# Forgetting attention with a gated FFN on one core: shared output chunks, stacked last tokens, a new order, and x of three batches turned by DMA

## The chip, the cores and the metric

One core of a Trainium2 chip runs the whole program. The metric is device time in microseconds, median of several runs. The five engines have instruction streams of their own: TensorE (PE, with its weight loads listed as PEld), VectorE (DVE), ScalarE (ACT), GpSimd (POOL) and SyncE (SP), which here only issues DMAs.

## The reference

For 8 batches, 8 heads, 576 tokens and a head dimension of 64, attention with a decay made from a gate `f`, and behind it an FFN with a gated convolution over the tokens:

```python
def _attn_ref(q, k, v, f):
    scores = scale * np.matmul(q, k.transpose(0, 1, 3, 2))
    cum = np.cumsum(np.log(np.clip(f, 0.0001, 1.0)), axis=-1)
    decay = cum[:, :, :, None] - cum[:, :, None, :]
    scores = np.where(causal, -1000000000.0, scores + decay)
    attn = softmax(scores)
    return np.matmul(attn, v)

def _moe_ref(x, w_in, conv_w, w_out):      # x: (8, 576, 512), the heads side by side
    h = np.maximum(x @ w_in, 0.0)          # d_ff = 1024
    conv_out = sum(conv_w[k] * shifted(h, k - 1) for k in range(3))
    gate = 1.0 / (1.0 + np.exp(-conv_out))
    return h * gate @ w_out
```

## The kernel before, in words

**Units of work.** Attention runs over 16 half batches `hb` (4 heads of a batch each), the FFN over 8 batches `b` and 8 blocks of 128 hidden features `ff`. The 576 tokens are four blocks of 128 and one of 64 (`SL`), the last tokens.

**Attention of a half batch.** q and k come transposed by DMA (L229, `q`), the rows of the decay are added to the operands (`rw`, `fi`), so that one matmul gives scores with decay. For each pair of heads, `sd` makes the four diagonal blocks, `so` the rest for one head, `st` the last 64 x 64 for all four (all in L362); `ed`, `eo`, `et` are the exponentials on ACT (L403, L420, L382). For half batches 0 to 7 a mask is added by a matmul (L370), for the rest POOL selects (`md`, `mt`: L406, L385). `va` casts v and adds a column of ones (L266, L268). `pv` (L438) multiplies: for query block n and head h it adds over key blocks m <= n, with the exponentials as weights (128 x 128) and 65 columns of v, so that the 65th column is the sum of the row. It has three parts of two, two and one query blocks, 12, 28 and 20 matmuls; the last query block is 128 rows wide and starts at token 448, so half of its rows repeat block 3. `n` (L445, L446) divides by the sums, in three parts. `t` turns the result by ten transposes on PE (L454) and `tx` copies it to `xt` on ACT or DVE (L459).

**FFN of a batch.** `f` (L468) is eight matmuls of 288 columns for one ff; `r` a relu on ACT (L478); `c` and `d` the convolution on DVE (L483, L485); `a` a tanh on ACT (L488); `g` the gate on DVE (L492). `o` (L499) multiplies with w_out: 128 tokens by 512 outputs, added over 8 ff. For the last 64 tokens (L503) the 512 outputs are split in two halves of 256, with 64-wide weights that go to two halves of the array, 16 matmuls a batch. `e` copies the result out of PSUM, `s` stores it, SP issuing (L525, L528).

**What sets the order.** Every task has a name such as `sd5` or `o3.2`; the string `ORDER` lists them all, some with the engine (`tx4@ACT`). `Plan.play` walks it and emits the instructions, so each engine's stream is the sub-sequence of its tasks, and the buffers (PSUM `ps`, 4; `xm`, 2; `xt`, 2; q/k `qk`, 4; and so on) are given out in that order. SP's queue is such a stream too: a DMA whose data aren't there yet holds all the DMAs behind it. Across engines only the semaphores of true dependences order the work.

**The start.** The gate `f` comes in two copies, one issued by ACT and one by SP (L271, L272); `dca`, `dcl`, `dcs`, `dck` make the decay and `ki` writes it to a DRAM image (L328). q and k of half batches 0 and 1 are loaded plain (`ld`, L208), turned on PE (`tp`, L215) and copied (`cl`, L221 on ACT, L223 on DVE).

Of the kernel before, what the change touches and what calls it, by code (L numbers as in the profile page):

```python
# [7 lines left out]
FP32 = mybir.dt.float32  # L8
FP16 = mybir.dt.float16
# [8 lines left out]
cw dca ld0 ld0.1.1 dcl dcs ld0.0.0 ld1 ld0.0.1 tp0.0.0 cl0.0.0@ACT cwt ld0.1.0 tp0.0.1 tp0.1.0 tp0.1.1 ld1.0.0 tp1.0.0  # L18
dck cl0.0.1@ACT cl0.1.0@DVE cl0.1.1@ACT cl1.0.0@ACT ld1.0.1 tp1.0.1 q2.0 cl2.0 cl1.0.1@ACT sd0 ed0 tp1.1.0 tp1.1.1
cl1.1.1@ACT ki@SP q2.1 sd1 so0.0 eo0.0 ed1 so1.1 eo1.1 so1.0 v0.0 v0.3 cl1.1.0@DVE rw1 so0.1 eo1.0 eo0.1 v0.4 v0.2  # L20
v0.1 sd3 ed3 so3.0 sd2 eo3.0 ed2 cl2.1 wi0 rw2 wi1 wic1@POOL so2.1 va1.0@DVE eo2.1 st0 et0 va0.0@DVE va0.1@DVE pv0.0
n0.0 so2.0 st1 et1 eo2.0 pv0.1 so3.1 pv0.2 eo3.1 va1.1@ACT sd5 q3.1 n0.1 n0.2 pv1.0 q3.0 wi3 n1.0 pv1.1 n1.1 pv1.2
n1.2 ed5 so5.1 eo5.1 cl3.1 wic0@POOL t0 tx0@ACT t1 tx1@DVE cl3.0 wi2 wic3@POOL q5.0 sd4 ed4 rw3 so4.1 eo4.1 f0.0 r0.0
f0.1 f0.2 f0.3 q5.1 v1.0 r0.1 v1.1 v1.2 v1.3 va2.0@POOL c0.0 d0.0 c0.1 wic2@ACT q4.1 r0.3 d0.1 so4.0 f0.4 c0.3 r0.2
c0.2 d0.3 eo4.0 h0 sd7 sd6 so5.0 a0.0 g0.0 a0.1 g0.1 r0.4 ed7 c0.4 d0.4 so7.0 eo5.0 cl5.1 so7.1 ed6 f0.5 cl5.0 a0.4
r0.5 v1.4 c0.5 rw5 eo7.1 wo1 st3 et3 eo7.0 a0.3 va2.1@POOL d0.2 woc1@POOL so6.0 d0.5 g0.4 st2 et2 f0.6 r0.6 eo6.0
so6.1 eo6.1 cl4.1 pv2.0 n2.0 pv2.1 va3.0@ACT a0.2 va3.1@ACT n2.1 f0.7 pv2.2 n2.2 g0.2 r0.7 c0.7 sd11 ed11 sd10 ed10
pv3.0 pv3.1 pv3.2 n3.0 so11.1 t2 n3.1 n3.2 q4.0 so10.1 wo2 d0.7 c0.6 cl4.0 a0.5 g0.5 eo11.1 wo0 eo10.1 tx2@ACT t3
tx3@ACT g0.3 d0.6 wo3 so11.0 eo11.0 a0.7 g0.7 so10.0 eo10.0 f1.0 f1.1 r1.0 c1.0 f1.2 d1.0 f1.3 q6.0 cl6.0 a0.6
woc2@POOL r1.1 st5 woc3@POOL r1.2 g0.6 rw4 et5 sd8 r1.3 c1.3 q6.1 woc0@ACT f1.4 q7.0 h1 a1.0 r1.4 sd9 ed9 d1.3 v2.0  # L30
o0.0 o0.1 so8.0 ed8 c1.4 cl6.1 d1.4 a1.3 c1.1 g1.3 a1.4 g1.4 cl7.0 g1.0 e0.0@ACT st4 et4 f1.5 eo8.0 r1.5 c1.5 d1.5
so8.1 eo8.1 so9.0 eo9.0 f1.6 f1.7 r1.7 so9.1 r1.6 v2.2 v2.1 v2.3 v2.4 eo9.1 va5.0@POOL va5.1@DVE va4.0@ACT rw6
va4.1@ACT pv5.0 pv5.1 pv5.2 n5.0 n5.1 n5.2 sd12 ed12 d1.1 c1.7 sd13 ed13 a1.1 pv4.0 n4.0 pv4.1 so12.1 pv4.2 t5 n4.1
n4.2 a1.5 so13.1 eo12.1 v3.0 v3.1 q7.1 t4 tx4@ACT o0.2 d1.7 tx5@DVE a1.7 c1.2 d1.2 g1.5 v3.3 eo13.1 q9.0 so12.0 eo12.0
o0.3 cl7.1 v3.2 a1.2 c1.6 d1.6 e0.1@ACT g1.1 a1.6 f2.0 r2.0 g1.7 g1.6 f2.1 f2.2 c2.0 r2.1 d2.0 rw7 g1.2 so13.0 r2.2
c2.2 eo13.0 o0.4 st7 et7 f2.3 sd15 q9.1 h2 a2.0 r2.3 e0.2@ACT va6.0@DVE va7.0@DVE so15.1 so15.0 pv6.0 zc ed15 eo15.1
f2.4 r2.4 eo15.0 v3.4 f2.5 sd14 q8.1 v4.0 so14.0 n6.0 c2.3 ed14 o1.0 st6 g2.0 eo14.0 d2.2 so14.1 a2.2 s0.2 o1.1
va6.1@DVE eo14.1 pv7.0 c2.1 et6 r2.5 e1.0@ACT fi9 d2.1 c2.4 d2.4 v4.2 d2.3 g2.2 a2.3 s0.1 q8.0 n7.0 f2.6 r2.6 sd18
sd19 ed19 c2.5 a2.4 pv6.1 pv6.2 d2.5 n6.1 n6.2 s1.0 fi8 g2.4 a2.5 va7.1@POOL pv7.1 pv7.2 v4.1 ed18 f2.7 n7.1 n7.2
q10.0 a2.1 g2.1 g2.3 r2.7 t6 so19.1 tx6@DVE c2.7 eo19.1 t7 v4.3 q11.0 tx7@ACT c2.6 d2.6 o1.2 f3.0 st9 md19 d2.7 f3.1  # L40
r3.0 a2.6 et9 o1.3 q11.1 c3.0 g2.6 r3.1 c3.1 a2.7 d3.1 st8 et8 sd17 e1.1@ACT ed17 f3.2 r3.2 md18 mt9 d3.0 g2.7 so19.0
# [67 lines left out]
def kernel(  # L109
# [601 lines left out]
```

## Time and profile before

| | us |
|---|---|
| three runs | 255.52, 256.81, 257.61 |
| median | 256.81 |
| span of the profiled execution | 254.4 |
| PE busy | 235.6 (93%) |
| ACT busy | 217.4 (85%) |
| DVE busy | 216.8 (85%) |
| POOL busy | 45.9 (18%) |

Of the profiled execution the page gives the span from its first instruction to its last, 254.4 us, and no other time; the runs' median stands beside it. The profile page gives for each engine the busy time, a line of 40 slices, the chain of work that ended last, and groups of instructions by line of the kernel. A group's mean duration of a matmul holds its latency; matmuls overlap one another, so steps between starts are shorter.

### The profile page before, as it was taken

What the parts mean: (1) busy time and instruction counts of PE and PEld (TensorE: products, weight loads), DVE (VectorE), ACT (ScalarE), POOL (GpSimd) and SP (SyncE); (2) the same over time, 40 slices, a digit from 0 to 9 for tenths busy, and PEclk for the clock granted to TensorE, in tenths of its full rate; (3) what the DMA queues carried; (4) which work ended last, traced back from release to release, by engine and by line L of the source; (5) the groups of instructions that cost most, each with busy time, mean ns of one, the idle gap of its engine ahead of it and who ended that gap; (6) DMA issues with size and microseconds to landing.
All of it is one profiled execution on the core that took longest, in us unless ns stands there. A gap on an engine that the chain in (4) does not pass through costs nothing.

```text
span 254.4 us, 6767 instructions
## 1 busy us (share of the span) xinstructions
PE 235.6 (93%) x2784; PEld 171.8 (68%) x2784; DVE 216.8 (85%) x353; ACT 217.4 (85%) x295; POOL 45.9 (18%) x79
## 2 busy tenths in 40 slices
PE   1899979779898999999999999999999999999992
PEld 1887766467656867687766886688767867875541
DVE  7631667969998999999989889889998999999961
ACT  4779858998999999897999799998999999796841
POOL 8100202022202401011104130245104302000000
PEclk9999999999999999999999999999999999999999
DMA  6979999999899979999998999999999802020335
GB/s 181 304 163 225 225 208 172 196 198 293 210 193 207 260 124 230 213 253 208 212 259 247 200 179 213 230 238 174 223 236 270 251 23 80 5 84 1 103 112 180
DMA packets 114695, 48.24 MB, mean 190 GB/s; under 512 B 104034, under 2 KB 105250, under 8 KB 114664
## 3 DMA queue, kind: packets, MB, share of 16 engines
q1 hardware_dynamic: 114370, 47.14, 85.4%
q8 instruction: 22, 0.36, 0.6%
q0 software_dynamic: 208, 0.51, 0.6%
q10 hardware_dynamic: 86, 0.16, 0.2%
q14 instruction: 9, 0.07, 0.1%
HBM read 21.11 MB, written 10.17 MB: 123 GB/s over the span
## 4 chain that ended last, share of the span: by engine, by line
PE 57%; DVE 15%; DMA 9%; SPq 7%; ACT 5%; issue 4%; POOL 0%; DVEq 0%; POOLq 0%; ACTq 0%
PE ps L468 14%; PE ps L499 14%; PE ps L362 12%; PE ps L438 9%; DVE u L483 5%; DVE hg L492 4%; SPq L258 4%; DMA vf<-in_v_dram 4%; DVE u L485 3%; DMA hg<-in_k_dram 3%; PE ps L454 2%; PE ps L503 2%; DMA qk<-in_k_dram 2%; ACT pp L420 2%; PE ps L370 2%
## 5 line engine op out<-in xcount | busy, mean ns | idle before, releaser
L420 ACT ACTIVATE pp<-ps 128x1024 f16<-128x1024 f32 x64 | 65.0, 1038 | 6.6 <-PE ps L362 4.9
L468 PE MATMUL ps<-xt,w_in_f 128*128 128x288 f16 x512 | 68.9, 286 | 1.8 <-ACT xt L459 0.8
L362 PE MATMUL ps<-qk 128*128 128x128 bf16 (+2 forms) x576 | 63.6, 240 | 1.6 <-ACT ht L478 1.1
L499 PE MATMUL ps<-w_out_f,hg 128*128 128x512 f16 x256 | 59.9, 379 | 0.1
L468 PEld LDWEIGHTS <-w_in_f 128*128 128x128 f16 x512 | 48.8, 98 | 15.8 <-issue 2.5
L483 DVE SCALAR_TENSOR_TENSOR u<-ht,cwt 128x576 f32<-128x576 f16 x64 | 54.8, 862 | 2.8 <-ACT ht L478 2.8
L485 DVE SCALAR_TENSOR_TENSOR u<-ht,cwt,u 128x576 f32<-128x576 f16 x64 | 52.9, 831 | 1.7
L362 PEld LDWEIGHTS <-qk 128*128 128x128 bf16 x576 | 40.7, 98 | 17.6 <-issue 3.6
L488 ACT ACTIVATE hg<-u,cw 128x576 f16<-128x576 f32 x64 | 49.0, 786 | 1.8 <-DVE u L485 1.5
L492 DVE SCALAR_TENSOR_TENSOR hg<-hg,ht 128x576 f16<-128x576 f16 x64 | 49.6, 804 | 0.8 <-ACT hg L488 0.8
L478 ACT ACTIVATE ht<-ps 128x576 f16<-128x576 f32 x64 | 41.2, 667 | 5.4 <-PE ps L468 4.6
L499 PEld LDWEIGHTS <-hg 128*128 128x128 f16 x256 | 24.2, 98 | 25.4 <-DVE hg L492 0.8
L438 PE MATMUL ps<-va,pp 128*128 128x65 f16 x896 | 33.5, 193 | 4.0 <-POOL va L266 1.8
L438 PEld LDWEIGHTS <-pp 128*128 128x128 f16 x896 | 32.1, 97 | 6.2 <-issue 3.2
L406 POOL TENSOR_SCALAR_AFFINE_SELECT pp<-pd 128x1024 f16<-128x1024 f32 x16 | 19.4, 1215 | 63.9 <-ACT pd L403 60.8
L446 DVE TENSOR_TENSOR xm<-ps,rc 128x512 f16<-128x512 f32 (+1 forms) x48 | 28.9, 603 | 1.7
L509 ACT COPY ob<-ps 128x1024 f32<-128x1024 f32 (+1 forms) x21 | 16.8, 800 | 2.4 <-PE ps L503 1.0
L403 ACT ACTIVATE pd<-ps 128x1024 f32<-128x1024 f32 x16 | 16.6, 1036 | 1.0 <-PE ps L362 0.8
L403 ACT ACTIVATE pp<-ps 128x1024 f16<-128x1024 f32 x16 | 16.2, 1038 | 1.3 <-PE ps L362 1.3
L235 DVE TENSOR_SCALAR qk<-qk,lim 128x2304 uint16<-128x2304 uint16 x12 | 10.4, 875 | 7.3 <-DMA qk<-in_k_dram 4.9
L370 PE MATMUL ps<-mask,ident 128*128 128x512 bf16 (+1 forms) x40 | 14.3, 358 | 0.7 <-ACT ht L478 0.4
L445 DVE RECIPROCAL rc<-ps 128x8 f32<-128x8 f32 (+1 forms) x48 | 9.3, 193 | 5.9 <-PE ps L438 4.9
(83 smaller groups left out, 186.3 us busy)
## 6 DMA issues: line engine op xcount, KB each, us to landing
vf<-in_v_dram SPq DMA_DIRECT2D x32, 256.0 KB, 4.7
out_dram<-ob SPq DMA_DIRECT2D x14, 512.0 KB, 3.1
qk<-blank SPq DMA_DIRECT2D x8, 540.0 KB, 6.7
ob<-in_moe_w_in_dram SPq DMA_DIRECT2D x4, 512.0 KB, 5.8
ob<-in_moe_w_out_dram SPq DMA_DIRECT2D x4, 512.0 KB, 6.4
vf<-in_v_dram SPq DMA_DIRECT2D x8, 128.0 KB
out_dram<-ob SPq DMA_DIRECT2D x16, 64.0 KB, 2.4
out_dram<-ob SPq DMA_DIRECT2D x4, 256.0 KB, 2.5
```

The lines of the kernel that those rows point to most:

```text
L362: nc.tensor.matmul(o, tk[:, h * S + k0:h * S + k0 + 128], tq[:, h * S + q0:h * S + q0 + n], start=first, stop=last and not by_matmul(hb, h))
L403: nc.scalar.activation(o, ps_of(f"sd{i}").rearrange("p (s c) -> p s c", s=2), AF.Exp, scale=SCALE)
L420: nc.scalar.activation(pair(i)[:, s, 512:1536], ps_of(f"so{i}.{s}"), AF.Exp, scale=SCALE)
L438: nc.tensor.matmul(o, block(hb, h, m, n), va[:, h, m, 0:D + 1], start=(m == 0), stop=(m == n))
L446: nc.vector.tensor_tensor(xm[:, 2 * u:2 * u + nj, :].rearrange("p j (h d) -> p j h d", d=D), got[:, :, :, 0:D], r.unsqueeze(3).broadcast_t ...
L468: nc.tensor.matmul(ps[:, MB + 288 * a:MB + 288 * (a + 1)], w_in_f16[:, cc, 128 * ff:128 * (ff + 1)], xt[:, cc, 288 * a:288 * (a + 1)], sta ...
L478: nc.scalar.activation(ht_of(b, ff)[:, 1:1 + S], ps_of(f"f{b}.{ff}")[:, MB:MB + S], AF.Relu, scale=0.5)
L483: nc.vector.scalar_tensor_tensor(u, ht[:, 0:S], cwt[:, ff, 0:1], ht[:, 1:1 + S], op0=ALU.mult, op1=ALU.add)
L485: nc.vector.scalar_tensor_tensor(u, ht[:, 2:2 + S], cwt[:, ff, 1:2], u, op0=ALU.mult, op1=ALU.add)
L488: nc.scalar.activation(hg_of(b, ff), u_t[slot[f"c{b}.{ff}", "u"]], AF.Tanh, scale=cw[:, ff, 1:2])
L492: nc.vector.scalar_tensor_tensor(hv, hv, 1.0, ht_of(b, ff)[:, 1:1 + S], op0=ALU.add, op1=ALU.mult)
L499: nc.tensor.matmul(ps[:, 512 * (c % 2):512 * (c % 2 + 1)], hg_of(b, ff)[:, 128 * c:128 * (c + 1)], w_out_f16[:, ff, :], **kw)
```

## The change

It has five parts.

- **Last 64 queries in pairs (`pv`, `norm`).** The last query block has 64 rows. Heads h and h + 2 go to the two halves of the array, 64-wide weights each, and to the upper and lower 64 partitions of the same columns. A half batch has then 18 groups of 65 columns instead of 20, 14 in the first part and 4 in the second; `n` has two parts (896 and 256 columns) instead of three. The tail exponentials `pt` lose their padding.
- **Stacked last tokens (`tails`, `ffn2`).** `k` copies the last 64 tokens of two batches side by side into `tl`; the last chunk of both batches together is one chunk of 128 tokens by 512 outputs, eight matmuls. For the last batch `k` is done ff by ff, on POOL, ACT or DVE.
- **x in two layouts joined (`turn`, `turned`, `ffn1`).** x of a half batch is 9 tiles of 128 x 128, the ninth with the last 64 tokens of both feature blocks. `f` has 512 + 64 columns instead of 2 x 288.
- **x by DMA (`turn_by_dma`).** For half batches 10 to 15 (`XD`) the transposes on PE and the copy are gone; a DMA transpose from `xm` to `xt`, issued by SP, takes their place.
- **Order and queues.** All of `ORDER` is new. The second gate copy is issued by ACT, `ki` by POOL; the constants get a tile of their own (`signs`); the last store's second half is issued by ACT.

```diff
-ORDER = """ cw dca ld0 ld0.1.1 dcl dcs ld0.0.0 ld1 ld0.0.1 tp0.0.0 cl0.0.0@ACT cwt ...
+ORDER = """ ld0 ld0.1.1 ld0.0.0 ld0.0.1 ld0.1.0 tp0.0.0 tp0.0.1 ld1 dca dcl tp0.1.0 ...
...
+    XD = (10, 11, 12, 13, 14, 15)
...
-    nc.sync.dma_start(fsb[BH:128], f.rearrange("b h s -> (b h) s"))
+    nc.scalar.dma_start(fsb[BH:128], f.rearrange("b h s -> (b h) s"))
...
-        for j, n in enumerate(((0, 1), (2, 3), (4,))[u]):
-            for h in range(HH):
-                o = ps[:, 512 * j + (D + 1) * h:512 * j + (D + 1) * (h + 1)]
-                for m in range(n + 1):
-                    nc.tensor.matmul(o, block(hb, h, m, n), va[:, h, m, 0:D + 1], start=(m == 0), stop=(m == n))
+        for j in range(SPLIT[u + 1] - SPLIT[u]):
+            n, h = group(SPLIT[u] + j)
+            c = 512 * (j // 7) + (D + 1) * (j % 7)
+            for m in range(n + 1):
+                if n < 4:
+                    nc.tensor.matmul(ps[:, c:c + D + 1], block(hb, h, m, n), va[:, h, m, 0:D + 1],
+                                     start=(m == 0), stop=(m == n))
+                else:
+                    for a in range(2):
+                        nc.tensor.matmul(ps[64 * a:64 * (a + 1), c:c + D + 1], block(hb, h + 2 * a, m, n),
+                                         va[:, h + 2 * a, m, 0:D + 1], start=(m == 0), stop=(m == n), skip_group_check=True)
...
+    def turn_by_dma(hb):
+        nc.sync.dma_start_transpose(xt_t[slot[f"tx{hb & ~1}", "xt"]][:, hb % 2, :].rearrange("p (x t) -> p x t", t=128),
+                                    xm_t[slot[f"n{hb}.0", "xm"]])
...
-            for a in range(2):
-                nc.tensor.matmul(ps[:, MB + 288 * a:MB + 288 * (a + 1)], w_in_f16[:, cc, 128 * ff:128 * (ff + 1)],
-                                 xt[:, cc, 288 * a:288 * (a + 1)], start=(cc == 0), stop=(cc == NCC - 1))
+            for c, x, n in ((0, 512 * (cc % 2), 512), (512, 1024 + SL * (cc % 2), SL)):
+                nc.tensor.matmul(ps[:, c:c + n], w_in_f16[:, cc, 128 * ff:128 * (ff + 1)], xt[:, cc // 2, x:x + n],
+                                 start=(cc == 0), stop=(cc == NCC - 1))
...
+    def tails(b, ffs, e):
+        t = tl_t[slot[f"k{b & ~1}", "tl"]][:, ffs[0]:ffs[-1] + 1, SL * (b % 2):SL * (b % 2 + 1)]
+        i = hg_t[slot[f"h{b}", "hg"]][:, ffs[0]:ffs[-1] + 1, S - SL:S]
+        {"ACT": nc.scalar.copy, "POOL": nc.gpsimd.tensor_copy, "DVE": nc.vector.tensor_copy}[e](t, i)
...
-            if c < 4:
-                nc.tensor.matmul(ps[:, 512 * (c % 2):512 * (c % 2 + 1)], hg_of(b, ff)[:, 128 * c:128 * (c + 1)],
-                                 w_out_f16[:, ff, :], **kw)
-            else:
-                for a in range(2):
-                    nc.tensor.matmul(ps[64 * a:64 * (a + 1), 0:256], hg_of(b, ff)[:, 512:576],
-                                     w_out_f16[:, ff, 256 * a:256 * (a + 1)], skip_group_check=True, **kw)
+            w = hg_of(b, ff)[:, 128 * c:128 * (c + 1)] if c < 4 else tl_t[slot[f"k{b & ~1}", "tl"]][:, ff, :]
+            nc.tensor.matmul(ps[:, 512 * (c % 2):512 * (c % 2 + 1)], w, w_out_f16[:, ff, :],
+                             start=(ff == 0), stop=(ff == NFF - 1))
...
+        if hb in XD:
+            add(f"tx{hb}", "SP", [f"n{hb}.{u}" for u in range(2)], lambda hb=hb: turn_by_dma(hb),
+                take=["xt"] if hb % 2 == 0 else [], give=[("xm", f"n{hb}.0")], behind=[f"tx{hb - 1}"] if hb % 2 else [])
+            continue
...
```

The new order at three places. First PE at the last query block of a half batch, values part of half batch 15 in both kernels. In the names `pp` are the exponentials of a pair of heads (99 and 100 before, 97 and 98 now, two pairs in each), `pt` those of the last block, `va` the values, and the number behind is what comes out, partitions by columns. Before:

```order
L438 LDWEIGHTS pp_99
L438 MATMUL ps_131<-va_94,pp_99 128x65
L438 LDWEIGHTS pt_103
L438 MATMUL ps_131<-va_94,pt_103 128x65
L438 LDWEIGHTS pp_100
L438 MATMUL ps_131<-va_94,pp_100 128x65
```

Now:

```order
L441 LDWEIGHTS pp_98
L441 MATMUL ps_133<-va_93,pp_98 128x65
L445 LDWEIGHTS pp_97
L445 MATMUL ps_133<-va_93,pp_97 64x65
L445 LDWEIGHTS pp_98
L445 MATMUL ps_133<-va_93,pp_98 64x65
```

All heads of one pair came one after another, in full width; now the last block's matmuls have 64-wide outputs and the two pairs of heads alternate, row by row.

Second, SP at the start, as the difference of the two (`vf` is the v tile, `hg` holds the plain q and k, `image` the decay rows in DRAM):

```order
+L258 DMA vf_89<-in_v_dram 128x8x64
+L208 DMA hg_129<-in_k_dram 128x2x576
+L229 DMA_TRANSPOSE qk_87<-in_k_dram 128x2304
 L229 DMA_TRANSPOSE qk_87<-in_q_dram 128x2304
-L328 DMA image<-kc 64x576 x3
-L229 DMA_TRANSPOSE qk_87<-in_k_dram 128x2304
-L258 DMA vf_89<-in_v_dram 128x8x64 x2
+L258 DMA vf_89<-in_v_dram 128x8x64 x3
 L251 DMA qk_86<-image 1x2304
```

The first v load stands ahead of both transposes, and the three writes of the decay rows are gone from SP.

Third, SP at batch 5, where `xt_118` is the turned x and `xm` the normalised values of half batches 10 and 11. Before, around the loads of half batch 14:

```order
L525 DMA out_dram<-ob_129 128x2x512
L229 DMA_TRANSPOSE qk_88<-in_q_dram 128x2304
L229 DMA_TRANSPOSE qk_87<-in_q_dram 128x2304
L258 DMA vf_89<-in_v_dram 64x8x64
L229 DMA_TRANSPOSE qk_87<-in_k_dram 128x2304
```

Now:

```order
L229 DMA_TRANSPOSE qk_87<-in_k_dram 128x2304
L258 DMA vf_89<-in_v_dram 128x8x64 x2
L467 DMA_TRANSPOSE xt_118<-xm_110 128x9x128
L537 DMA out_dram<-ob_130 128x2x512
L467 DMA_TRANSPOSE xt_118<-xm_109 128x9x128
L258 DMA vf_89<-in_v_dram 64x8x64
L537 DMA out_dram<-ob_132 128x2x512
L229 DMA_TRANSPOSE qk_87<-in_q_dram 128x2304
```

Two transposes of x stand among the loads, and the rest of v and the q of half batch 14 come behind the second of them.

More of the change, by code (lines that the diff above doesn't have):

```diff
@@ L655 @@
             for ff in range(NFF):
+                add(f"k{b}.{ff}", "POOL/ACT/DVE", [f"g{b}.{ff}"], lambda e, b=b, ff=ff: tails(b, [ff], e),
+                    behind=[f"k{b - 1}"])
                 for c in range(NKB):
[L657 removed]
+                    add(f"o{b}.{c}.{ff}", "PE", ([f"g{b}.{ff}"] if c < 4 else [f"k{b - 1}", f"k{b}.{ff}"]) + (wo if ff == 0 else []),
                         lambda b=b, c=c, ff=ff: ffn2(b, f"o{b}.{c & ~1}.0", c, [ff]),
```

192 lines of the change are left out of this document (98 added, 94 removed).

## The prediction

> **What bounds the kernel now.** I read the page's busy times first, then the same by stage (the windows view), then the chain of waits.
>
> ```profile
> span 254.4 us, 6767 instructions
> PE 235.6 (93%) x2784; PEld 171.8 (68%) x2784; DVE 216.8 (85%) x353; ACT 217.4 (85%) x295; POOL 45.9 (18%) x79
> ```
>
> ```profile
> 0.00:12.40 12.40, 6.37 (x62) 5.85 (x63) 8.61 (x30) 7.01 (x7) 6.74 (x35) 1.00 0.85 242
> 12.40:42.30 29.90, 27.26 (x380) 21.68 (x377) 14.29 (x24) 23.07 (x28) 3.49 (x3) 1.00 1.01 205
> 42.30:82.30 40.00, 34.57 (x384) 24.76 (x385) 37.15 (x54) 38.62 (x54) 6.06 (x7) 1.00 1.04 211
> 82.30:203.00 120.70, 120.59 (x1533) 89.83 (x1533) 113.42 (x182) 112.99 (x158) 27.82 (x33) 1.00 1.06 223
> 203.00:254.40 51.40, 46.81 (x432) 29.68 (x429) 43.30 (x66) 35.74 (x53) 1.77 (x3) 0.99 0.21 73
> ```
>
> The columns after a stretch and its length are busy us of PE, weight loads, DVE, ACT and POOL, the granted clock, the DMA share and GB/s. From 82.3 us on PE never stops (120.59 of 120.70), at full clock, with DVE and ACT at 94% behind it. So in the 172 us after 82.3 a microsecond of PE work removed is a microsecond of time, as long as DVE and ACT lose as much and the DMA rings, whose share is above 1 until 203 us, still deliver in time. Before 82.3 us PE idles 6.0 + 2.6 + 5.4 = 14.1 us: that part is paced by loads, as two pieces of the chain show:
>
> ```profile
> 21.48 3.96 DMA vf<-in_v_dram
> 25.52 1.31 DVE va L266 x2
> ...
> 49.54 5.61 DMA qk<-in_k_dram
> ```
>
> A matmul's printed duration contains its latency; what it takes of PE is the step from one to the next, which the chain gives for whole runs (start, us, matmuls):
>
> ```profile
> 87.83 0.64 PE ps L438 x20
> 88.47 0.56 PE ps L454 x10
> 89.02 0.44 PE ps L362 x4
> 89.46 0.56 PE ps L454 x10
> 90.02 1.73 PE ps L499 x8
> ...
> 97.28 0.99 PE ps L503 x16
> ...
> 98.61 0.98 PE ps L468 x8
> ```
>
> So 0.032 us for 65 columns (L438), 0.056 for 128 (L454), 0.216 for 512 (L499), 0.122 for 288 (L468); the four off-diagonal scores (64+448+320+192 columns) take 0.44, which leaves 0.03 for the one of 64. The 16 of L503 have 256 columns each but 64-wide weights: two stand side by side in the array, eight pairs in 0.99. Going into that mode and out of it costs extra, seen alone at the start, where one 64-wide matmul stands between full ones:
>
> ```profile
> 24.96 0.19 PE L362 MATMUL ps<-qk 128*128 128x64 bf16 x1
> 25.09 0.22 PE L365 MATMUL ps<-sel_k,kc 128*64 128x64 bf16 x1
> 25.23 0.20 PE L367 MATMUL ps<-kc,sel_q 128*128 128x64 bf16 x1
> 25.27 0.19 PE L362 MATMUL ps<-qk 128*128 128x64 bf16 x1
> ```
>
> The steps are 0.13 and 0.14 us in place of 0.03 each: 0.21 for the trip.
>
> **The change part by part**, against the profiled 254.4 us.
>
> *PE, turning.* 160 transposes become 10 half batches of 9: 70 x 0.056 = -3.9.
>
> *PE, last output chunk.* 8 batches x (0.99 + 0.10 to enter the mode) = 8.7 become 4 x 8 x 0.216 = 6.9 in full width: -1.8. The copies `k` that stack the tails mostly run on POOL, which is busy 18%; if one came late, one chunk of 1.73 would wait.
>
> *PE, values of the last 64 queries.* 20 full matmuls of 65 columns (0.64) become ten side-by-side pairs with 64-wide weights plus a trip into the mode and back, once a half batch; in the order, shown with the change, the two heads of a pair alternate. At the least a pair costs what one 65-column matmul does: 10 x 0.032 + 0.21 = 0.53, or -1.8 in 16 half batches. At the most the two don't overlap: 0.64 + 0.21, +3.4. Which it is depends on how fast 64-wide weights follow one another. L503's steady steps can't tell, since 256 columns cover the load; its first four loads can:
>
> ```profile
> 97.21 0.14 PEld L503 LDWEIGHTS <-hg 128*64 128x64 f16 x4 [0.21 <-issue]
> ```
>
> ```profile
> L503 PEld LDWEIGHTS <-hg 128*64 128x64 f16 x128 | 6.4, 109 | 2.7 <-issue 2.6
> ```
>
> Four loads of 109 ns lie within 140, so two pairs started some 0.03 us apart. I take 0.04 a pair: 0.61, -0.5. [...]
>
> *PE, first FFN matmul.* 512 + 64 columns in place of 2 x 288: 0.216 + 0.03 against 0.245, nothing; were the short one 0.04, as after a mode change above, 256 of them would add 2.6.
>
> PE's sum: -3.9 - 1.8 - 0.5 = **-6.2** (from -7.5 to +0.3 with every end taken).
>
> *DVE and ACT* must lose as much, or they take over.
>
> ```profile
> L446 DVE TENSOR_TENSOR xm<-ps,rc 128x512 f16<-128x512 f32 x32 | 22.1, 692 | 1.1
> L446 DVE TENSOR_TENSOR xm<-ps,rc 128x256 f16<-128x256 f32 x16 | 6.8, 425 | 0.6
> L445 DVE RECIPROCAL rc<-ps 128x8 f32<-128x8 f32 x32 | 6.5, 203 | 4.3 <-PE ps L438 3.4 <-ACT pp L420 0.8
> L445 DVE RECIPROCAL rc<-ps 128x4 f32<-128x4 f32 x16 | 2.8, 175 | 1.6 <-PE ps L438 1.4
> L266 DVE CAST va<-vf 128x1024 f16<-128x1024 f32 x8 | 5.5, 711 | 5.2 <-DMA vf<-in_v_dram 5.2
> L459 ACT COPY xt<-ps 128x1152 f16<-128x1152 f16 x7 | 7.7, 1118 | 2.3 <-PE ps L454 2.3
> L459 DVE COPY xt<-ps 128x1152 f16<-128x1152 f16 x9 | 6.6, 753 | 1.4 <-PE ps L454 1.2
> L509 ACT COPY ob<-ps 128x1024 f32<-128x1024 f32 x14 | 14.2, 1013 | 0.8 <-PE ps L499 0.8
> L221 ACT ACTIVATE qk<-ps,lim 128x1152 uint16<-128x1152 uint16 x6 | 7.5, 1309 | 1.9 <-PE ps L215 1.9
> ```
>
> The normalisation is 38.2 us now. With 896 + 256 columns, at the slope (692 - 425) / 256 = 1.04 ns a column, it is 16 x (1.09 + 0.43 + 0.25 + 0.18) = 31.2: -7.0. Two copies of x fewer (-1.5), three casts of v fewer (-2.1), two output copies of 1024 columns more (2 x 1.2, by the same slope): DVE -8. ACT: four copies of x fewer (-4.5), two of q/k (-2.6), two output copies (-2.0), and shares of the tails about even: -9. Both lose more than PE does, so PE's sum stands; had they lost nothing, 6.2 would have had to come out of their 7 us of idle time in the dense stretch.
>
> *Start.* The second gate copy leaves SP's queue, the decay rows go out by POOL, the first v load comes before the two transposes. SP no longer holds loads behind the decay rows. The first gate copy's row on SP is 0.59 us, and every load behind it moves up by that:
>
> ```profile
> 0.80 0.59 SPq L272 DMA_DIRECT2D u<-in_f_dram  x1
> ...
> 12.07 1.79 SPq L328 DMA_DIRECT2D image<-kc  x3
> ```
>
> 0.6 is offered for certain; with the 1.8 of L328 it would be 2.4. On POOL a transfer into the same image takes longer to land, but its reader comes late:
>
> ```profile
> image<-pd POOLq DMA_DIRECT2D x3, 72.0 KB, 5.5
> ```
>
> ```profile
> 18.78 0.35 SPq L251 DMA_DIRECT2D qk<-image  x1
> ```
>
> Issued once the rows are made, well before the 12.07 of today, it is there by then. I take -1.5 and, since the whole order of the first 82 us is new and 14.1 us of idle time lie there, -5 to +4.
>
> *x turned by DMA.* Six transfers of half a q transpose's size join SP's queue.
>
> ```profile
> qk<-in_q_dram SPq DMA_TRANSPOSE x14, 9.3
> qk<-in_k_dram SPq DMA_TRANSPOSE x14, 5.6
> ```
>
> ```profile
> 122.34 5.78 SPq L229 DMA_TRANSPOSE qk<-in_k_dram  x2
> ```
>
> On SP, behind the second of batch 5, stand v, an output and the q of half batch 14 (the rows shown with the change), all of which wait with it. Between the last normalisation and the first FFN matmul of its batch, PE's order has two output chunks (1.73 each), scores and a values part: 5.3 us in batch 5, 5.4 in batch 6, and four chunks, 6.9, in batch 7. At half of 5.6 to 9.3 us x lands in 2.8 to 4.7, inside all three. At the full 9.3 it is late by 4.0, 3.9 and 2.4: 10.3. So 0 to 10.3; nearer to the half size, but behind other transfers while the DMA share is above 1: 0.75 each in batches 5 and 6, none in 7, when the rings are nearly empty: +1.5. The added transfer time is 6 x 5.78 / 4 = 8.7 us of ring time, of which four fall before 203 us.
>
> **Sum:** 254.4 - 6.2 - 1.5 + 1.5 = 248.2 us of span. The median of the runs, 256.81, lies 2.4 above this span; 248.2 + 2.4 = **250.6 us**.
>
> **The rivals.**
>
> *x comes late* (the slower one). The transfers take as long as those of twice the size, PE stops at the first FFN matmul of batches 5, 6 and 7, and q of half batch 14 is held behind on SP. For: the DMA share above 1, an in-order SP. Against: SP itself often waits for PE, not for rings:
>
> ```profile
> SPq L229 <- PE ps L362: 17.5, 5, 5.5
> ```
>
> Price 10.3 in place of 1.5: 250.6 + 8.8 = 259.4. It decides once the three stalls together use up the 7.7 us gained elsewhere, at a landing of about 8.4 us.
>
> *The new order opens holes.* DVE and ACT have 6% to spare in the dense stretch and PE idled 5.4 in 40 us just before it. Holes of 5% over 120.7 us are 6.0: 256.6, no gain. Against: both side engines get 8 to 9 us lighter.
>
> *The pairs of 64-wide weights don't overlap*: 16 x (0.64 + 0.21 - 0.64) = +3.4 in place of -0.5: 254.5. For: no row has such short pairs, and one 64-wide matmul alone cost 0.14. Against: the four loads within 0.14 us.
>
> *The start gains more*: -5 with no wait for x: 250.6 - 3.5 - 1.5 = 245.6.
>
> **How the numbers follow.** Forecast 0.52; x late 0.09; holes 0.13; dear pairs 0.11; better start 0.15. A measurement of this kernel can tell about 1% from no change, so 254.2 and 259.4 are the borders. Faster: 0.52 + 0.15, half of the 0.11, less 0.02 for the forecast's own spread: 0.71; same: the holes and the rest, 0.20; slower: 0.09. The range reaches from the better start to the holes: 245.5 to 257.0.
>
> **What would show it.** Right: L454's kind at 90 transposes, PE busy near 229, idle below 82 us down by a microsecond or two, PE still without gaps from there on, L445's runs of 20 near 0.4 us and 0.2 for the mode. Wrong: PE waiting for DMA into xt at the first FFN matmul of batches 5 to 7; runs of L445 at 0.6 or more; a windows table whose middle stretch has PE below 97%; the first scores no earlier than before.

## The result, and the profile after

The changed kernel takes 254.84 us (median of 14 runs, the lowest 250.93) and the kernel before 256.26 beside it; the ratio is 0.9844, with a 95% interval of 0.9808 to 0.9880. It is faster, inside the range, but by less than the 6.2 us of the sum: 4.0 us by the ratio, 1.4 by the medians, 2.6 by the means (253.69 and 256.29) when three outliers are left out, 271.84 and 598.33 us now and 307.48 before. The ratio leaves out runs more than 1.5% above the fastest of their kernel, eight of the fourteen now and one before, and the profiled execution, 254.81 us, is one of the eight: so 4.0 is the favourable end, and the profile shows costs that not every run pays.

The page of the changed kernel, span and busy times:

```profile
span 253.1 us, 6392 instructions
PE 230.6 (91%) x2618; PEld 146.2 (58%) x2618; DVE 215.3 (85%) x322; ACT 209.3 (83%) x285; POOL 60.2 (24%) x92
```

PE lost 5.0 us of busy time and the span only 1.3. The stages of the prediction, with the same columns:

```profile
0.00:12.40 12.40, 4.43 (x44) 4.01 (x45) 7.61 (x23) 5.76 (x5) 7.20 (x34) 1.00 0.91 245
12.40:42.30 29.90, 28.59 (x380) 21.48 (x380) 14.05 (x25) 20.08 (x23) 3.63 (x4) 0.94 0.96 190
42.30:82.30 40.00, 34.72 (x395) 21.83 (x394) 38.36 (x52) 36.69 (x51) 10.26 (x12) 1.00 1.07 229
82.30:203.00 120.70, 117.44 (x1457) 76.02 (x1455) 113.36 (x163) 111.07 (x155) 33.68 (x35) 0.99 1.07 217
203.00:253.10 50.10, 45.40 (x350) 22.86 (x348) 41.89 (x63) 35.72 (x55) 5.46 (x8) 0.99 0.37 118
```

Length less PE's busy time is PE's idle time:

| stage | before | forecast | after |
|---|---|---|---|
| 0 to 82.3 us | 14.1 | 12.6 | 14.6 |
| 82.3 to 203 us | 0.1 | 1.6 | 3.3 |
| 203 us to the end | 4.6 | 4.6 | 4.7 |

So idle time grew by 3.7 us where the forecast had none added. And the granted clock, full in the dense part before, is 0.94 and 0.99 in two stages. Both have one place each.

**The start.** The first pieces of the chain of waits:

```profile
1.39 5.69 DMA u<-in_f_dram
7.18 0.47 DVE u L567
7.68 0.69 ACT u L312
```

The second gate copy, now behind the first on ACT's queue, is issued at 1.39 and there at 7.08. The clip of the gate starts at 7.18; the same instruction before stood here:

```profile
4.28 0.44 DVE L554 TENSOR_SCALAR u<-u 128x576 f32<-128x576 f32 x1
```

That is 2.9 us later, and with it come later the decay, the copies of q and k and, by 1.5 us, the first scores (13.98 instead of 12.44).

**The hole.** SP's queue between 161 and 180 us (L229 the transposes of k and q, L467 those of x):

```profile
161.04 4.74 SPq L229 DMA_TRANSPOSE qk<-in_k_dram  x1
165.82 1.20 SPq L258 DMA_DIRECT2D vf<-in_v_dram  x2
167.07 3.04 SPq L467 DMA_TRANSPOSE xt<-xm  x1
170.22 0.51 SPq L537 DMA_DIRECT2D out_dram<-ob  x1
170.82 1.66 SPq L467 DMA_TRANSPOSE xt<-xm  x1
...
173.98 3.76 SPq L229 DMA_TRANSPOSE qk<-in_q_dram  x1
...
179.87 0.91 SPq L243 DMA_DIRECT2D qk<-blank  x1
```

and the chain from there:

```profile
173.98 5.88 DMA qk<-in_q_dram
...
179.87 6.46 DMA qk<-blank
...
186.43 1.04 PE ps L359 x12
```

Each row of SP is a transfer and how long SP is held by it. x of batch 5 is in time here. The q of half batch 14 stands behind it and is issued at 173.98; the fill of its other rows (`blank`, then the decay rows) can only follow at 179.87, when the q has landed, and PE, which wants the scores of half batch 14 from about 183.8 us on, waits until 186.43:

```profile
PE ps L359 <- DMA qk<-blank: 2.6, 1, 2.6
```

**The clock.** Stretches of 3.41 us about the hole; the granted clock is the column after POOL's:

```profile
183.93:187.35 3.42, 0.92 (x14) 0.82 (x15) 1.37 (x2) 0.77 (x2) 0.00 (x0) 1.00 1.21 170
187.35:190.76 3.41, 3.41 (x69) 3.25 (x67) 2.04 (x4) 2.38 (x3) 1.10 (x1) 0.50 1.08 208
```

After the stretch in which PE was busy 0.92 of 3.42 us comes one at half clock, in which 3.41 us of busy time do 1.7 us of work: the 32 products of 65 columns that start at 188.53 take 1.76 us to the next task, and those that start at 178.82 take 1.00. A second lies at the start, from 13.27 to 16.68. Ahead of that, PE's first matmuls run at half pace in both kernels, though the clock column shows 1.00 there. These are the first 18 transposes before and the first 36 now:

```profile
6.54 2.10 PE L215 MATMUL ps<-ident_b,hg 128*128 128x128 bf16 x18 [1.11 <-DMA hg<-in_q_dram]
```

```profile
6.57 3.89 PE L215 MATMUL ps<-ident_b,hg 128*128 128x128 bf16 x36 [6.57 <-DMA hg<-in_q_dram]
```

Transposes start 0.107 us apart up to 11.35 us before and up to 9.85 now, and 0.056 apart from there on. Until then PE is busy for 5.45 and 3.17 us, which costs about 2.7 and 1.6 us.

**The books** of this execution: the half clock costs about 1.6 + 2 x 1.7 = 5.0 us now and 2.7 before, 2.3 more. So PE's work fell by 5.0 + 2.3 = 7.3, and -7.3 + 2.3 + 3.7 idle = -1.3, which is the span.

### The profile page after: what moved, and what is told of

It reads as the page before. It is cut to its first block, busy times and chain, and to the rows that moved or that the text cites. A ratio compares the mean times of both kernels' runs of the same rounds, so it can differ in the third digit from the quotient of the medians.

```text
span 253.1 us, 6392 instructions
## 1 busy us (share of the span) xinstructions
PE 230.6 (91%) x2618; PEld 146.2 (58%) x2618; DVE 215.3 (85%) x322; ACT 209.3 (83%) x285; POOL 60.2 (24%) x92
## 4 chain that ended last, share of the span: by engine, by line
PE 57%; DVE 15%; DMA 13%; ACT 6%; issue 4%; SPq 2%; POOL 0%; ACTq 0%; DVEq 0%
PE ps L516 21%; PE ps L481 15%; PE ps L359 9%; PE ps L441 6%; DMA qk<-in_q_dram 5%; DVE u L496 4%; DVE u L498 3%; ACT pp L417 3%; DMA qk<-blank 3%; DVE hg L505 2%; DMA qk<-in_k_dram 2%; DMA u<-in_f_dram 2%; PE ps L445 2%; DVE xm L455 1%; PE ps L367 1%
## 5 line engine op out<-in xcount | busy, mean ns | idle before, releaser
L481 PE MATMUL ps<-xt,w_in_f 128*128 128x512 f16 (+1 forms) x512 | 69.3, 286 | 2.1 <-POOL w_in_f L559 1.6
L359 PE MATMUL ps<-qk 128*128 128x64 bf16 (+2 forms) x576 | 63.9, 242 | 4.5 <-DMA qk<-blank 2.6
L498 DVE SCALAR_TENSOR_TENSOR u<-ht,cwt,u 128x576 f32<-128x576 f16 x64 | 56.2, 895 | 0.7
L481 PEld LDWEIGHTS <-w_in_f 128*128 128x128 f16 x512 | 34.3, 98 | 31.3 <-POOL w_in_f L559 1.9
L441 PE MATMUL ps<-va,pp 128*128 128x65 f16 x640 | 25.0, 196 | 1.4 <-ACT pp L417 1.2
L455 DVE TENSOR_TENSOR xm<-ps,rc 128x896 f16<-128x896 f32 (+1 forms) x32 | 24.2, 758 | 1.1
L441 PEld LDWEIGHTS <-pp 128*128 128x128 f16 x640 | 23.0, 99 | 3.7 <-ACT pp L417 1.1
L510 POOL COPY tl<-hg 128x512 f16<-128x512 f16 (+1 forms) x9 | 5.9, 669 | 45.6 <-DVE hg L505 45.6
L453 DVE RECIPROCAL rc<-ps 128x14 f32<-128x14 f32 (+1 forms) x32 | 6.6, 206 | 11.5 <-PE ps L441 7.7
L266 POOL CAST va<-vf 128x1024 f16<-128x1024 f32 x7 | 8.5, 1226 | 25.9 <-PE ps L359 11.6
```

The lines of the kernel that those rows point to most:

```text
L359: nc.tensor.matmul(o, tk[:, h * S + k0:h * S + k0 + 128], tq[:, h * S + q0:h * S + q0 + n], start=first, stop=last and not by_matmul(hb, h))
L441: nc.tensor.matmul(ps[:, c:c + D + 1], block(hb, h, m, n), va[:, h, m, 0:D + 1], start=(m == 0), stop=(m == n))
L455: nc.vector.tensor_tensor(x.rearrange("p (j h d) -> p j h d", j=a, d=D), got[:, :, :, 0:D], r.unsqueeze(3).broadcast_to((128, a, g, D)), o ...
L481: nc.tensor.matmul(ps[:, c:c + n], w_in_f16[:, cc, 128 * ff:128 * (ff + 1)], xt[:, cc // 2, x:x + n], start=(cc == 0), stop=(cc == NCC - 1))
L498: nc.vector.scalar_tensor_tensor(u, ht[:, 2:2 + S], cwt[:, ff, 1:2], u, op0=ALU.mult, op1=ALU.add)
```

## The experiments

Theory: PE's work fell at least as forecast, and the gain went into the late gate, into the q of half batch 14 behind x on SP, and into the clock behind PE's gaps. Rivals: the hole has another cause; what is gained is waited for elsewhere, since three engines are close to one another. Times are medians beside runs of the kernel before on the same chip; the changed kernel, run again beside the second group, took 254.08 (ratio 0.9859, 0.9791 to 0.9928; before 255.70).

**c0_changed**, the changed kernel again.

> The changed kernel once more, as the measure for the three kernels timed beside it on the same chip. Every theory expects its median again, 252 to 256 us, and in its trace one hole of 2 to 3 us on TensorE between the last value chunk and the scores of half batch 14, near 183 us.

254.08 us, span 253.6 in the profile. The hole is there, but cut in two by the border of the stretches:

```profile
183.76:187.18 3.42, 2.17 (x18) 0.98 (x15) 3.38 (x5) 2.57 (x4) 0.00 (x0) 1.00 1.09 255
187.18:190.59 3.41, 2.42 (x64) 2.23 (x65) 0.90 (x4) 1.72 (x2) 0.63 (x1) 1.00 1.24 178
```

With 2.17 and 2.42 us busy, no half clock follows, in the second of them or after it. The same program pays for the same hole here its length alone, and 2.6 + 1.7 us in the other profile. Its span is no shorter for that: in the dense stretch PE idles 5.0 us here, as it also waits 2.0 for the rows of an earlier half batch, before 160 us, and 0.7 for x of batch 5. The books of this execution are -6.4 of work, +0.6 for the clock and +5.0 idle, -0.8 in all. How much of the idle time one execution shows is therefore no fixed number.

**e1_gate_sp**, the second gate copy back on SP.

```diff
-    nc.scalar.dma_start(fsb[BH:128], ...)
+    nc.sync.dma_start(fsb[BH:128], ...)
```

> The second gate copy goes back to the head of SP's queue; all else is the changed kernel. Theory (the copy on ScalarE's queue lands late: the clip of the gate started at 7.18 us in place of 4.28, the copies of q and k on ScalarE queue behind the logarithm, the first scores start at 13.98 in place of 12.44 and PE's idle time before them costs a window of 3.4 us at half clock): the clip starts near 4.3, scores at 12.5 or before, no half-clock window there, and the time falls by 1.5 to 3 us, to about 249 to 250. Rival (the first 80 us are paced by the loads and by ScalarE, so an earlier start is lost again before 82 us): the first scores are earlier, the time stays within 0.7 us of the changed kernel's 252.

253.71 us beside 256.14 (0.9891, 0.9830 to 0.9952). The clip is early again:

```profile
4.68 0.54 DVE L567 TENSOR_SCALAR u<-u 128x576 f32<-128x576 f32 x1 [0.31 <-DMA u<-in_f_dram]
```

and PE idles 11.9 us up to 82.3 us, 2.6 less than in the changed kernel's profile; but the time can't be told from the changed kernel's. The first scores come at 13.00 us, not at 12.5 as the theory had it, and PE stays at half pace until 15.4 us here (18 transposes from 11.10 on take 2.10 us): with 9.2 us of busy time that costs 4.6 us, against the 1.6 + 1.7 of the changed kernel's start. So half of what the earlier gate gave goes to the clock in this profile, and the run doesn't price the gate.

**e15_later_gate_warm** goes further: gate on SP, the order of e10 (below), and work for PE from 3.7 us on.

```diff
-ld0.1.0 tp0.0.0 tp0.0.1 ld1
+ld0.1.0 wu0 wd0 wu1 wd1 tp0.0.0 tp0.0.1 ld1
...
-    for x in range(0):
+    for x in range(2):
```

> The kernel of e10_scores_later, with the gate's second copy back on SyncE's queue and with eight products of an identity, 512 columns each and read by nobody, ahead of TensorE's first transposes, so that TensorE is busy 3 to 4 us earlier. Theory (TensorE's gaps before 15 us cost clock beside time: the half-clock stretch to about 16 us would be worth up to 2 us of TensorE work): the granted clock is full from 12 us on or earlier, the first 42 us end 1 to 2 us sooner than in e10_scores_later and nothing later takes it back, 250 to 252.5 and the fastest of the study. Rival (the first 82 us are paced by loads, ScalarE and VectorE; what TensorE gains it waits for near 45 us): the wait near 45 us grows by as much, the time within 1 us of e10_scores_later, 253.5 to 255.5.

253.48 us beside 256.29 (0.9872, 0.9832 to 0.9912), between the two ranges and at the edge of the rival's. One of PE's waits below 60 us, in e15 and then in e10_scores_later:

```profile
PE ps L481 <- POOL w_in_f L559: 2.1, 1, 2.1
```

```profile
PE ps L481 <- POOL w_in_f L559: 0.4, 1, 0.4
```

PE is at full pace from 8 us on (36 transposes from 7.15 on take 2.65 us, 3.89 in the changed kernel), and waits 1.7 us longer for the FFN weights near 44 us, with a half-clock stretch behind that (the granted clock is 0.96 from 42.3 to 82.3 us). By 82.3 us PE has done 823 matmuls in e15, without the eight that nobody reads, and 825 in e10: what it gained at the start is given back by then.

**e2_q14_early**, the q of half batch 14 ahead of x on SP.

```diff
-tx10 c4.7 o3.3
+q14.0 tx10 c4.7 o3.3
```

> In the order the q transpose of half batch 14 stands ahead of the two transposes of x of batch 5 on SP; nothing else is moved. Theory (x did not come late itself, but q of half batch 14 waited behind it on SP, so its fill landed at 186.3 us and PE stood still for 2.8 us at 183.6, with a half-clock window behind it): the hole at the scores of half batch 14 goes, and the time falls by 2.5 to 4.5 us, to 248 to 249.5. Rival (the DMA rings are full, so the order on SP only decides who is late): x of batch 5 or the fill of half batch 15 comes late instead, a hole of 1.5 to 3 us stands elsewhere after 160 us, and the time stays within 1 us of the changed kernel's.

255.90 us beside 256.14 (0.9862, 0.9785 to 0.9939): no faster than the changed kernel, as the rival had it. SP's rows and PE's only wait between 165 and 185 us:

```profile
167.86 4.10 SPq L229 DMA_TRANSPOSE qk<-in_q_dram  x1
172.06 1.33 SPq L467 DMA_TRANSPOSE xt<-xm  x1
...
174.11 1.68 SPq L467 DMA_TRANSPOSE xt<-xm  x1
```

```profile
PE ps L481 <- DMA xt<-xm: 2.8, 2, 2.1
```

The hole is now at the first FFN matmuls of batch 5, 2.1 us in one piece and 2.8 in all. The order on SP chooses who is late. **e5_both** joins e1 and e2.

> The gate copy back on SP and the q transpose of half batch 14 ahead of x, together. If both theories hold, the gains add: 4 to 6.5 us below the changed kernel, 246 to 248. If only one holds, this run equals that one's within 0.7 us. If both rivals hold, it stays at 251 to 253.

255.67 us (0.9979, 0.9940 to 1.0017), with the same hole at the FFN, 3.1 us. That is e2's time and above the 251 to 253 that both rivals together had. With the q ahead of x, nearly all of the gain over the kernel before is gone; why a hole of this size costs more there than in its old place is not shown.

**e9_x_twice** adds two turning DMAs, into a spare tile.

```diff
+        if hb in (10, 11):
+            nc.sync.dma_start_transpose(spare..., xm_t[slot[f"n{hb}.0", "xm"]])
```

> The turning DMAs of x of half batches 10 and 11 are issued twice each, the second time into a spare tile that nobody reads: it adds two transposing DMAs to SyncE's queue and takes nothing away. Theory (between 160 and 187 us the path of the turning DMAs is the short resource, and the queries of half batch 14 wait behind x): each extra one holds the queries 1.7 to 3 us longer, the hole near 183 us grows to 5 to 8 us, the time is 3 to 5 us over the changed kernel. Rival (the hole has another cause and SyncE has slack there): the hole stays at 2 to 3 us and the time within 1 us of the changed kernel.

258.48 us beside 255.70 (1.0076, 1.0035 to 1.0118), 4.4 over the changed kernel on that chip. PE's waits from 155 to 195 us:

```profile
PE ps L360 <- DMA out_dram<-ob: 4.3, 1, 4.3
PE ps L360 <- DVE xm L456: 1.9, 1, 1.9
PE ps L484 <- DMA xt<-xm: 0.8, 1, 0.8
```

The wait of 4.3 is the scores of half batch 14 (L360 here); the profile names a store as its end, issued at 184.95, right behind the fill of the q's other rows (183.25) and the decay rows (184.20). The hole grew by 1.7, from 2.6 to 4.3, less than to the 5 to 8 expected; x was late by 0.8, much as in c0_changed, and the time rose as expected: this path has no slack. SP's rows give the size: from the issue of the k of half batch 14 to that of its q pass 16.5 us here with four DMAs of x between them, 12.9 in the changed kernel with two, and 9.3 in e3 below with none, so each puts the q back by 1.8 us. The wait of 1.9 for DVE at 160 us lies ahead of the spare transfers and is not explained by them; e4_half_cols has it too. **e13_x_act** was to tell SP's queue from the transfers, by issuing x from ACT.

```diff
-        nc.sync.dma_start_transpose(xt_t...
+        nc.scalar.dma_start_transpose(xt_t...
```

> The six turning DMAs of x are issued from ScalarE's queue instead of SyncE's, at the same places of the order; size and number of transfers stay. Theory A (SyncE's queue is the short thing: it is held 1.3 to 4.7 us by each transposing DMA, and the queries of half batch 14 stand behind two of x): SyncE issues those queries 3 to 5 us earlier and the hole near 183 us goes; ScalarE is held 1.3 to 3 us by each of the six instead, and its group work is late by as much: hole under 0.7 us there, new waits for ScalarE, the time between 252 and 258. Theory B (the transfers themselves, not the issuing queue, are the limit: the DMA engines are busy all the time up to 203 us): the queries land as late as before, hole still 2 us or more, and ScalarE's hold comes on top, 256 or more.

261.68 us (1.0179, 1.0122 to 1.0236). It can't decide, because in its trace the q on SP waits for x, whose DMA ACT now issues:

```profile
SPq L229 <- DMA xt<-xm: 5.9, 1, 5.9
```

SP issued the q of half batch 14 at 178.53, when x, under way for 3.70 us from 174.81 on, had landed. Whether SP's hold or the transfers are the limit stays open.

**e3_pe_turn**: x of all six half batches on PE again, at the same places.

```diff
-    XD = (10, 11, 12, 13, 14, 15)
+    XD = ()
-tx10 ... tx11 ...
+t10 tx10@DVE ... t11 tx11@ACT ...
```

> x of half batches 10 to 15 is turned on PE again (nine transposes and a copy on VectorE or ScalarE, at the places where the DMA stood); all else is the changed kernel. Theory (the transfers of x cost more on SP than they save on PE): no hole at half batch 14, PE busy up by 54 transposes x 0.056 = 3.0 us, and the time is equal or up to 2 us lower than the changed kernel's. Rival (turning by DMA pays in full and the hole comes from the rest of SP's queue): the hole stays and the time is 3 us or more above the changed kernel's, near 255.

260.85 us beside 256.14 (1.0199, 1.0149 to 1.0249). The hole at half batch 14 is gone, as the theory had it, and its q is issued at 171.34 instead of 173.98; but the time rose, as the rival had it, and by more. PE starts those scores at 186.42, no sooner than the changed kernel with its hole (186.43), since the 54 transposes, 3.0 us, come back with waits, of which these are from 165 to 245 us:

```profile
PE ps L481 <- ACT xt L472: 1.1, 2, 0.7
PE ps L462 <- DVE xt L472: 0.9, 1, 0.9
PE ps L481 <- ACT p L379: 0.9, 1, 0.9
```

In this order, turning by DMA is worth some 6 us by the medians, not the 3.0 of its matmuls. **e7_x5_pe** does so for half batches 10 and 11 alone, **e8_x5_pe_gate** with the gate on SP too.

```diff
-    XD = (10, 11, 12, 13, 14, 15)
+    XD = (12, 13, 14, 15)
-pv11.1 q14.1
+pv11.1 t10 tx10@DVE q14.1
-sd27 o3.2
+sd27 t11 tx11@DVE o3.2
```

> The x of half batches 10 and 11 is turned on TensorE again, as before the change; those of 12 to 15 stay with the DMA. Theory (four turning DMAs in a row on SyncE hold back the queries' transpose of half batch 14, and the 2.8 us hole near 183 us is that): two of the four are gone, so the queries of half batch 14 land 3 to 5 us earlier, the hole shrinks to under 0.5 us, the half-clock stretch behind it goes too (about 1.7 us); TensorE pays 12 transposes at about 0.06 us and two switches of operation, 1.0 us. In sum 2 to 3 us under the changed kernel, 250 to 252. Rival (the keys and queries are late because VectorE and ScalarE norm them late, or because the DMA rings are full in any order): the hole stays at 2 us or more and the time is that of the changed kernel plus 1 us.

> The kernel of e7_x5_pe with the gate's second copy back on SyncE's queue. Theory (the late gate costs about 2 us before 15 us, but in the runs of e1_gate_sp the gain did not last to the end): the start is 1 to 2 us shorter, and with the hole gone too the end is 0.5 to 2 us under e7_x5_pe, 249 to 251. Rival (what the start gains is waited for later at the loads of the first 82 us): same as e7_x5_pe within 0.7 us.

257.90 (1.0104, 1.0070 to 1.0137) and 258.00 us (1.0090, 1.0062 to 1.0118) beside 255.70: both expectations fell. The hole at half batch 14 is gone in both, but not because its q comes sooner: e7 issues it at 174.39, and PE reaches those scores only at 192.73. PE's waits in e7 from 160 to 195 us:

```profile
PE ps L481 <- ACT pd L400: 2.1, 1, 2.1
PE ps L516 <- DVE xt L472: 0.9, 1, 0.9
PE ps L359 <- DVE xt L472: 0.9, 1, 0.9
PE ps L481 <- DVE xm L455: 0.6, 1, 0.6
```

Behind each turning on PE the next task waits 0.9 us for the copy of x on DVE, and an exponential on ACT is late by another 2.1. The 18 transposes (the expectation said 12) are 1.0 us; its two switches of operation were an estimate that no step shows: 24 scores take 1.45 us to the first transpose behind them (173.26 to 174.71), and 1.45 to an output product in the changed kernel (168.70 to 170.15), where the step from the last transpose back to a product is 0.06. With 1.8 + 2.1 + 0.6 of these waits, less the 2.2 of the hole and the 0.7 for x that c0_changed waits in the same stretch, that is +2.6 of the 3.8 measured. The waits for the copies cost more than the transposes.

**e10_scores_later** fills the hole instead: the scores of half batch 14 go behind two value chunks on PE.

```diff
-md27 sd28 r5.5 c5.4 so28.0 ed28 mt13 pv12.1 n12.1 eo28.0 c5.3 pv13.0
+md27 r5.5 c5.4 mt13 pv12.1 n12.1 c5.3 pv13.0 sd28 so28.0 ed28 eo28.0
```

> Only TensorE's order changes: the scores of the diagonal blocks of half batch 14 (sd28, with the products of their weights, so28.0, ed28, eo28.0) go behind the last value chunk of half batch 12 and the first of half batch 13, so that about 2.5 us of TensorE work that waits for nothing stands where the 2.8 us hole is. No DMA is moved. Theory (the hole is work put ahead of queries that SyncE cannot bring earlier): the hole shrinks to under 0.7 us and the half-clock stretch behind it goes, 2 to 4 us under the changed kernel, 250 to 252. Rival (all three engines are within a few per cent of each other there, as putting x back on TensorE showed, where the hole went and others came): the wait is found again within 20 us, on the values or on half batch 14's later blocks, and the time is the changed kernel's within 1 us.

254.43 us beside 256.36 (0.9834, 0.9754 to 0.9913): as the rival had it. From 155 to 205 us PE now waits

```profile
PE ps L359 <- DMA qk<-image: 0.9, 1, 0.9
PE ps L359 <- DVE xm L455: 0.7, 1, 0.7
...
PE ps L359 <- DMA qk<-blank: 0.2, 1, 0.2
```

and the dense stretch as a whole is about as full as the changed kernel's:

```profile
82.30:203.00 120.70, 117.21 (x1455) 74.97 (x1456) 112.69 (x164) 112.01 (x155) 33.78 (x36) 1.00 1.08 221
```

3.5 us idle, against 3.3 and, in c0_changed, 5.0: the wait at this place is spread, and the whole is not smaller than two executions of one program differ. No version beats the changed kernel by what can be told.

**e4_half_cols** asks what sets the pace of the 64-wide pairs.

```diff
-ps[64 * a:64 * (a + 1), c:c + D + 1], ..., va[:, h + 2 * a, m, 0:D + 1]
+ps[64 * a:64 * (a + 1), c + (32 if m else 0):c + D + 1], ..., va[:, h + 2 * a, m, (32 if m else 0):D + 1]
```

> For the last 64 queries of each half batch, the products with the value blocks after the first (line 445) take 33 of their 65 columns; the sums of the other 32 columns are left out, so that part of the output is not computed. Weights, their loads and the number of products stay. It tells what sets the 0.033 us at which the pairs of products with 64-wide weights follow each other. Theory (the pair's 65 columns at full clock set it, 0.027 us and a few ns, and the loads of the weights run beside it): steps fall to 0.018 to 0.022 us, and a half batch's run of 20 pairs from 0.65 with its edges to about 0.45. Rival (the load of a 64-wide block of weights sets it): steps stay at 0.03 us or more. The time of the whole kernel changes by less than 3 us either way.

A run of 20 in the changed kernel, and in e4 with half the columns in 16 of them:

```profile
86.04 0.44 PE ps L445 x20
```

```profile
84.31 0.42 PE ps L445 x20
```

A column takes 0.216 us / 512 = 0.42 ns, 65 of them 0.027 us, so eight pairs with 32 columns fewer would have saved 0.11 us, had columns set the pace; 0.02 came. My theory fell: the columns don't set the pace here. Whether the two 64-wide loads do, or a fixed step of a pair, this run can't part; either way two loads fit in 0.032 us, as four pairs start from 89.27 to 89.40 us in the changed kernel. The single time, 253.23 us, is that of the changed kernel within 3 us, as both expected. Its trace shows one thing more: order and DMAs are the changed kernel's, and yet no hole stands at half batch 14. The q is issued at 172.81, and PE, after 1.9 us of waiting for DVE near 160 us and a half-clock stretch behind that, comes to those scores only at 185.4, when they are ready. The time was lost ahead of the hole instead of in it.

## Why the prediction was right in sign and wrong in size

The range held, but its width did that: 254.84 us lies nearer to the figures of two rivals, 254.5 and 256.6, than to 250.6. By the forecast's own border for faster, 254.2, the ratio (252.3 us) lies on one side and the median on the other. In the two profiles PE's work fell as forecast, and idle time and clock took most of it back.

**PE's work: right in sum.** The transposes are 80 + 10 as said, and the output chunk is at full width. The term mis-sized is the pairs, at its cheap end:

```profile
88.74 0.41 PE L441 MATMUL ps<-va,pp 128*128 128x65 f16 x8
89.09 0.32 PE L445 MATMUL ps<-va,pp 128*64 128x65 f16 x8
89.24 0.20 PE L445 MATMUL ps<-va,pt 128*64 128x65 f16 x2
89.27 0.29 PE L445 MATMUL ps<-va,pp 128*64 128x65 f16 x8
89.40 0.20 PE L445 MATMUL ps<-va,pt 128*64 128x65 f16 x2
89.53 0.29 PE L462 MATMUL ps<-ident,xm 128*128 128x128 f16 x2
```

Eight full products and 20 in pairs take 89.53 - 88.74 = 0.79 us, trip included; 28 full ones at 0.032 took 0.90. That is -0.11 a half batch, -1.8 in sum instead of -0.5. Two 64-wide loads together fit in 0.032 us: four pairs start from 89.27 to 89.40. With -1.8 the three terms are -7.5; the books show -7.3 in one execution and -6.4 in the other, beside the -6.2 forecast. That the pairs gave 1.3 more than taken offset a part of the losses below, and that was luck.

**The start: the step that failed is "I take -1.5".** It counted what SP's queue gains by giving the copy away and not when the copy lands on the queue that takes it: clip at 7.18 instead of 4.28. Idle time to 82.3 us grew by 0.5 instead of shrinking by 1.5. What of it the gate itself costs at the end can't be told: e1 and e15 mended it, and their times are the changed kernel's within what is measurable.

**x by DMA: "inside all three" was right, "+1.5" was the wrong victim.** x of batches 5 to 7 lands in time in the profile, and 0.7 us late for batch 5 in c0_changed. The price is paid by the transfer that the text named as queued behind it, the q of half batch 14, which was counted under the slower rival only, not in the sum: 2.6 us of wait, 3.3 of idle time in the dense stretch instead of 1.6 (5.0 in c0_changed). e2, e3 and e9 show that it is x's DMAs that hold the q; no run shows that the time is won back when they don't. Whether -3.9 has the right size stays open: e3 lost some 6 us for 54 of the 70 transposes, as PE also waited for copies, but with x put back into an order that was not made for it; the kernel before, with all of x on PE, idled 0.1 us in the dense stretch.

**The clock was not in the sum at all:** 2.3 us more than before in the profiled execution, 0.6 in c0_changed. **DVE and ACT.** "DVE -8" failed: DVE lost 1.5, ACT 8.1 of its 9. The normalisation came as reckoned (L453 and L455 30.8 us, 31.2 said), but the two q/k copies that ACT lost went to DVE, which the step left out, and the same convolution takes longer:

```profile
L498 DVE SCALAR_TENSOR_TENSOR u<-ht,cwt,u 128x576 f32<-128x576 f16 x64 | 56.2, 895 | 0.7
L223 DVE TENSOR_SCALAR qk<-ps,lim 128x1152 uint16<-128x1152 uint16 x4 | 5.8, 1472 | 3.0 <-PE ps L215 3.0
```

Before, the first was 52.9 us, 831 ns each, and the second 3.0 us for two. Why the first slowed wasn't tried. So DVE lost far less than PE's work did, against "Both lose more than PE does". DVE, at 94% of the dense stretch, is as full there as before; it is one of the engines that PE waits for in e3, e7 and e10. The 2.4 us outside of the span are 1.7 in every run since; the rest was spread between runs.

**The rivals.** *Holes* came, one of 2.6 us and not 5% throughout. *x late* is half true: the mechanism, with another victim and a quarter of the price. *Dear pairs* fell. *Better start* fell.

## What to carry to other kernels

When a transfer is put on an in-order queue, price the transfer behind it, and then the first instruction that needs that one, in the sum and not only as a rival; when a transfer is taken off a queue, look up when it lands on the new one. Here PE, DVE and ACT were busy for 97, 94 and 92% of the dense stretch, with a DMA share of 1.07, and moving one wait bought little: four edits that closed the hole each showed waits again elsewhere. A PE gap is to be priced with the clock behind it, 2.6 + 1.7 us in one profile here and 2.2 + 0 in another.

## What the runs showed of the hardware

In the profile of the changed kernel the granted clock changes, up to PE's last matmul, at 13.27, 16.68, 187.35 and 190.76 us: the two stretches at half clock are 3.41 us long each, and 187.35 - 16.68 is 50 times 3.413. Seven stretches of that length behind the slow start, by PE's busy time in them, and the granted clock of the stretch that follows:

| run | stretch, us | PE busy, us | clock of the next |
|---|---|---|---|
| e9_x_twice | 184.92 to 188.33 | 0.00 | 0.50 |
| changed kernel | 183.93 to 187.35 | 0.92 | 0.50 |
| changed kernel | 43.98 to 47.39 | 1.78 | 1.00 |
| kernel before | 31.83 to 35.25 | 1.84 | 1.00 |
| changed kernel | 9.85 to 13.27 | 1.93 | 0.50 |
| c0_changed | 183.76 to 187.18 | 2.17 | 1.00 |
| c0_changed | 187.18 to 190.59 | 2.42 | 1.00 |

Of these seven, half clock followed the two emptiest and not the two fullest; between them the busy time of a stretch alone doesn't tell. The emptiest, in e9:

```profile
184.92:188.33 3.41, 0.00 (x0) 0.00 (x0) 1.24 (x2) 0.40 (x1) 0.00 (x0) 1.00 0.98 262
188.33:191.74 3.41, 2.81 (x40) 2.40 (x40) 0.00 (x0) 1.70 (x2) 0.60 (x1) 0.50 1.06 209
```

In the profile of the changed kernel 2.50 us of the hole lie in one stretch, and it cost another 1.7; in c0_changed 1.25 and 0.99 lie on the two sides of the border at 187.18, and it cost nothing more. By an estimate from these two profiles, runs of one program can differ by 1.7 us through the place of that border alone.

That the spread of the 14 runs comes from this was not tried alone, and the clocks of the runs bear it out in part. One stretch at half clock lowers the mean granted clock of a run by about 0.007, an estimate: half of 3.41 us in 253. Without the two outliers, the four runs at 0.995 or more took 250.93 to 253.37 us and the two at 0.985 or less 254.81 and 254.88; but the six at 0.989 to 0.992 took anything from 251.64 to 255.87.
